# Transposing query weights straight from DRAM, modulation weights by columns, first key products in halves, and a new hand-written order

## The chip, the core and the metric

The kernel runs on one core of a Trainium2 chip. The core has TensorE (PE in the profile, its weight loads PEld), VectorE (DVE), ScalarE (ACT), GpSimd (POOL) and SyncE (SP), each working through its own queue of instructions in order, and 16 DMA engines that carry the transfers which SP (and at the very start ACT) issues. The metric is the device time of one execution in microseconds.

## What is computed

A transformer block with adaptive layer norm: linear attention with softmax features for 2,048 tokens of width 512 in 32 heads of 16, and a gated MLP of width 1,376. All inputs are bf16.

```python
mod = (_silu(c) @ w_mod).reshape(c.shape[0], 6, 1, -1)
sa, ca, ga, sb, cb, gb = ...
h = _layernorm(x) * (1 + ca) + sa
q, k, v = split(h @ wqkv)                          # 32 heads of 16
pq, pk = q @ w_phi, k @ w_phi                      # head by head
phi_q = concat(softmax(pq), softmax(-pq)); phi_k = concat(softmax(pk), softmax(-pk))
kv = einsum('bhsf,bhsd->bhfd', phi_k, v); z = phi_k summed over s
o = (phi_q @ kv) / (phi_q @ z + 1e-6)
x = x + ga * (o @ wo)
h = _layernorm(x) * (1 + cb) + sb
x = x + gb * ((sigmoid(h @ w_gate) * (h @ w_up)) @ w_down)
```

## The kernel before

Tokens are worked on in 16 tiles of 128. Nothing is scheduled at run time: every piece of work is a named task, and the text `ORDER` lists all tasks. The program is emitted in that order, so each engine's queue holds its own tasks in the order of the text. A suffix (`@A`, `@D`, `@P`) moves a task to ACT, DVE or POOL; without one it goes to the first engine that its `G.add` names. Buffers (eight PSUM banks, and slots for the larger SBUF tiles) are handed out in the order of the text too, so a task can wait for an earlier user of its bank.

The head of the kernel, with the names that the rest uses:

- **Loads** (`ld_...`, L664 to L687) stand in SP's queue. `ld_x0a` to `ld_x3a` bring the tokens, `ld_wk0/1`, `ld_wv0`, `ld_wq0` the three parts of `A_wqkv` into `wqk_sb` and `wv_sb`, `ld_wm00/01` the shift and scale columns (0 to 1,023) of `w_mod` for the first norm, each load with two of the four blocks of 128 rows; `ld_wmga` and `ld_wmm2` its other columns. In the built program a load is not issued before the eighth load ahead of it has landed. ACT issues two small loads, of `c` and `w_phi`.
- **Warm-up** (`warm0`, `warm1_0` to `warm1_15`, L720): matmuls on zeros that keep PE running while the loads come.
- **Norm of the tokens**: `st1_t` (statistics, DVE, L799), `rs1_g`, `nmr1_g`, `xn1_t` (normalized tile, L824 to L828). Tiles are grouped: group 0 is tile 0, group 1 tile 1, group 2 tiles 2 and 3, then two tiles to a group.
- **Transposes of the tokens**: `tphgj` (PE, L841) transposes column block j (of four) of group g, and `hm1_gj` (L848 on ACT, L850 on DVE or POOL) scales and shifts it into `h1T`. Groups 6 and 7 are transposed by DMA instead (`xT1_t`, L833). `hm1` needs the modulation column `modc`, which `modc1.0`, `modc1.1` (PE, 16 small matmuls each, L735) and `modc1c` (ACT, L741 and L742) make of the two loads.
- **Folded weights**: `w_phi` is multiplied into Wq and Wk once. For Wk, `tpw` (PE, L759) transposes, `wTc` (L763) copies into `wT_sb`, `fold1j` (L776) multiplies with the block-diagonal `bd`, `foldc1j` (L782, L784) copies to `wqk_f`. For Wq the transposes are DMAs (`wqT0` to `wqT3`, L769) from `wqk_sb`, then `fold0j`, `foldc0j`. In both, a fold waits for all four transposed blocks.
- **Keys and values**: `Kt` (four matmuls over the four blocks j, L867) and `Vt` (L871) of tile t; `et` (two exponentials, ACT, L883), `nt` (sums, DVE, L886), `rt` (reciprocal), `phit` (POOL or DVE, L889), `vat` (copy of the values, L907), `kvt` (eight matmuls that add tile t to `kvacc`, L280).
- **Queries**: `Qcb` (L945) and their exponentials `qecb` (L950), where the order finds room. `modca` (from `ld_wmga`, read back over DRAM as `gra`, and multiplied into `wo`) and `modc2` (from `ld_wmm2`) make the other modulation columns.

After the keys come `kvm`, `kvp`, `kvz`, `kvn`, the attention output per tile (`sm`, `num`, `u`, `o`, `oT`, `out`), the second norm, and the MLP in six chunks (`g`, `tg`, `u`, `hm`, L574 to L595; `y`, `fin`, `st`, L612 to L621).

In the order before, each engine's queue starts so (names as above; what is not needed is left out):

```
PE   warm0 c1 warm1_0..7 tpw1 tpw0 tpw3 warm1_8 tpw2 warm1_9..14 fold11 fold13 fold12 fold10 modc1.0 modc1.1 tph20 tph21 tph11
     tph22 warm1_15 tph03 tph23 tph10 tph01 tph00 K2 tph02 tph13 K3 tph12 tph33 tph30 K0 tph32 V2 K1 tph53 V3 tph52 tph31 modca.0 modca.1 V0 V4
SP   x0b x0a x1a wk0 wk1 x2a wm00 wm01 x2b wv0 x1b wq0 wd2 wmga x3a wqT2 wqT0 wqT3 wqT1 xT1_10 xT1_11 gwa wu1 wmm2 xT1_13 xT1_12 wg0 wo wu0 wd gra
```

Of the kernel before, what the change touches and what calls it, by code (L numbers as in the profile page):

```python
# [1133 lines left out]
```

## Time and profile before

| | us |
|---|---|
| median of 3 runs | 208.01 |
| lowest and highest | 207.98, 208.36 |
| the profiled execution | 208.63 |
| its span in the profile | 206.9 |

The profiled execution's own time is 1.7 us longer than the span from its first to its last instruction. The profile page gives the busy time of each engine, a strip of 40 slices, and the chain of waits: the work that ended last, followed back. The other views used are the busy time of each engine in chosen stages, what each engine waited for, the instructions in order of time (start, duration, engine, line, operation, output and inputs, count; in brackets the idle time before and what ended it), and the list of transfers (issuing queue, count, size, and the time from issue to landing).

### The profile page before, as it was taken

Reading aid. Unit: us, or ns where it says so; the run is one execution under the profiler, and the core shown is the slowest. Engines: PE = TensorE matmul, PEld = TensorE weight load, DVE = VectorE, ACT = ScalarE, POOL = GpSimd, SP = SyncE. Lnnn points to the kernel's source line nnn. Section 1 sums busy time; section 2 is a strip of 40 time slices with the busy share of each in tenths; the row PEclk is TensorE's granted clock in tenths of the full one; section 3 lists DMA queues with packets and bytes.
Section 4 is the critical chain, followed back from the end, with each engine's and each line's share of the span. In section 5 each row is a group of like instructions: output and inputs, shape, how many; then the busy total and the mean of one; then the engine's idle time right before and its main releaser. Section 6 shows DMA issues by size and latency. Waiting matters only on the chain.

```text
span 206.9 us, 4373 instructions
## 1 busy us (share of the span) xinstructions
PE 199.4 (96%) x1539; PEld 112.8 (54%) x1563; DVE 168.8 (82%) x462; ACT 110.1 (53%) x267; POOL 96.3 (47%) x128
## 2 busy tenths in 40 slices
PE   7889999999999999999999999999999999999993
PEld 2465554554676689768764544454444444444442
DVE  3999999998989998999999999898797865235632
ACT  2689999999979986433343543231523351144100
POOL 5787999999976987774256000014400220000000
PEclk9999999999999999999999999999999999999999
DMA  6999877697101211205321121141223022000111
...
DMA packets 32557, 19.27 MB, mean 93 GB/s; under 512 B 21169, under 2 KB 30738, under 8 KB 32530
## 3 DMA queue, kind: packets, MB, share of 16 engines
...
q8 instruction: 14, 0.23, 0.5%
q14 instruction: 13, 0.11, 0.2%
q10 hardware_dynamic: 530, 0.02, 0.1%
...
## 4 chain that ended last, share of the span: by engine, by line
PE 71%; ACT 18%; DMA 4%; DVE 3%; SPq 2%; issue 1%; DVEq 0%; ACTq 0%
PE y_ps L612 18%; PE u_ps L574 17%; PE g_ps L574 17%; ACT e L883 8%; PE a_ps L483 7%; PE q_ps L945 4%; ACT h1T L848 4%; DMA wmod_sb<-in_w_mod_dram 4%; ACT vaug L907 3%; PE num L366 2%; PE num L450 2%; DVE phi L889 1%; PE g_ps L576 1%; SPq L664 1%; DVE ks L886 1%
## 5 line engine op out<-in xcount | busy, mean ns | idle before, releaser
L584 ACT ACTIVATE tg<-g_ps 128x512 bf16<-128x512 f32 (+5 forms) x66 | 28.9, 454 | 58.0 <-PE g_ps L574 38.1
L612 PE MATMUL y_ps<-wd_sb,wmod_sb 128*128 128x512 bf16 (+4 forms) x184 | 43.8, 366 | 0.2
L595 DVE SCALAR_TENSOR_TENSOR wmod_sb<-tg,u_ps 128x512 bf16<-128x512 bf16 (+4 forms) x63 | 30.0, 494 | 15.0 <-ACT tg L584 7.3
L574 PEld LDWEIGHTS <-wu_sb 128*128 128x128 bf16 (+1 forms) x252 | 21.7, 99 | 15.7 <-issue 0.2
L574 PEld LDWEIGHTS <-wg_sb 128*128 128x128 bf16 (+1 forms) x252 | 21.5, 99 | 14.7 <-issue 0.2
L889 POOL TENSOR_TENSOR phi<-e,ks 128x1024 bf16<-128x1024 bf16 (+2 forms) x17 | 27.7, 1637 | 1.1 <-DVE ks L899 0.3
L612 PEld LDWEIGHTS <-wmod_sb 128*128 128x128 bf16 (+1 forms) x187 | 17.4, 98 | 16.9 <-issue 0.2
L574 PE MATMUL u_ps<-wT_sb,wu_sb 128*128 128x512 bf16 (+2 forms) x122 | 23.7, 321 | 0.1
L574 PE MATMUL g_ps<-wT_sb,wg_sb 128*128 128x512 bf16 (+2 forms) x122 | 23.7, 321 | 0.1
L503 POOL TENSOR_SCALAR ve<-mv 128x2 f32<-128x2 f32 (+1 forms) x8 | 1.8, 223 | 42.3 <-DVE mv L493 42.3
L574 PE MATMUL u_ps<-wqk_sb,wu_sb 128*128 128x128 bf16 (+4 forms) x127 | 19.9, 287 | 0.1
L886 DVE TENSOR_REDUCE ks<-e 128x64 f32<-128x1024 bf16 (+2 forms) x22 | 19.7, 903 | 0.3 <-ACT e L883 0.2
L574 PE MATMUL g_ps<-wqk_sb,wg_sb 128*128 128x128 bf16 (+4 forms) x127 | 19.6, 287 | 0.1
L883 ACT ACTIVATE e<-k_ps 128x512 bf16<-128x512 f32 (+2 forms) x44 | 18.4, 500 | 0.0
L950 ACT ACTIVATE eT<-q_ps 128x512 bf16<-128x512 f32 x32 | 16.8, 611 | 1.8 <-PE q_ps L945 1.7
L474 POOL TENSOR_TENSOR o<-u 128x512 bf16<-128x512 f32 x10 | 12.6, 1269 | 9.5 <-DVE u L456 4.2
L619 DVE TENSOR_TENSOR ot<-y_ps,x 128x512 bf16<-128x512 f32 (+2 forms) x17 | 11.2, 656 | 6.9 <-PE y_ps L612 6.6
L483 PE MATMUL a_ps<-wo_sb,oT 128*128 128x512 bf16 x57 | 15.7, 379 | 0.4
L945 PE MATMUL q_ps<-h1T,wqk_f 128*128 128x512 bf16 x62 | 15.7, 379 | 0.1
L867 PE MATMUL k_ps<-wqk_f,h1T 128*128 128x512 bf16 x63 | 15.5, 379 | 0.1
L871 PE MATMUL v_ps<-wv_sb,h1T 128*128 128x512 bf16 x59 | 15.2, 379 | 0.2
L799 DVE BATCH_NORM_STATS2 st<-x_sb 128x6 f32<-128x512 bf16 x16 | 10.8, 673 | 2.6 <-DMA x_sb<-in_A_x_dram 2.6
...
## 6 DMA issues: line engine op xcount, KB each, us to landing
...
wmod_sb<-in_w_mod_dram SPq DMA_DIRECT2D x3, 512.0 KB, 6.5
wmod_sb<-in_w_mod_dram SPq DMA_DIRECT2D x1, 1536.0 KB, 10.3
...
```

The costliest lines, as they stand in the source:

```text
L483: pe.matmul(ap_[:], lhsT=oT[:, j, :], rhs=wo_sb[:, j, :], start=(j == 0), stop=(j == KT - 1))
L574: pe.matmul(ps[:fsz, 0:n], lhsT=w[:, j, ft * P:ft * P + fsz], rhs=h[:, j, 0:n], start=(j == 0), stop=(j == KT - 1))
L584: G.add(f"tg{k}.{ft}", {"ACT": 0.13 + n * 0.00083}, lambda e, tg=tg, g_ps=g_ps, fsz=fsz, n=n: act.activation(tg[:fsz, 0:n], g_ps[:fsz, 0:n ...
L595: dve.scalar_tensor_tensor(hm_all[:fsz, hm[k].slot, ft, 0:n], tg[:fsz, 0:n], 1.0, u_ps[:fsz, 0:n], op0=ALU.add, op1=ALU.mult)
L612: mm = pe.matmul(y[:, 0:c1 - c0], lhsT=hm_all[:fsz, hm[k].slot, ft, tl * P:(tl + 1) * P], rhs=wd_sb[:fsz, ft, c0:c1], start=(ft == 0), sto ...
L867: pe.matmul(kp[:], lhsT=h1T[:, j, t * P:(t + 1) * P], rhs=wqk_f[:, j, D:2 * D], start=(j == 0), stop=(j == KT - 1))
L871: pe.matmul(vp[:], lhsT=h1T[:, j, t * P:(t + 1) * P], rhs=wv_sb[:, j, :], start=(j == 0), stop=(j == KT - 1))
L883: act.activation(ee[:, ha:hb, s, :], kp[:, ha * DH:hb * DH].rearrange("p (h j) -> p h j", j=DH), ACT.Exp, scale=1.0 - 2.0 * s)
L886: dve.tensor_reduce(ks[:, ha:hb].rearrange("p h s -> p (h s)"), ee[:, ha:hb].rearrange("p h s j -> p (h s) j"), axis=AX.X, op=ALU.add)
L889: engine(e).tensor_tensor(ph[:, ha * 32:hb * 32].rearrange("p (h j) -> p h j", j=DH), ee[:, ha:hb].rearrange("p h s j -> p (h s) j"), ks[: ...
L945: pe.matmul(qp[:], lhsT=wqk_f[:, j, blk * P:(blk + 1) * P], rhs=h1T[:, j, cq * 512:(cq + 1) * 512], start=(j == 0), stop=(j == KT - 1))
L950: act.activation(eT[cq][:, s * 4 + blk, :], qp[:], ACT.Exp, scale=1.0 - 2.0 * s)
```

## The change

- `DIRECT = [1, 0]`: the load of Wq into `wqk_sb` is gone. The four DMA transposes `wqT0` to `wqT3` read the rows of `A_wqkv` in DRAM. Wk is still loaded and transposed by PE.
- Wk is loaded in halves of rows, not of columns. `tpwk` transposes the four column blocks of row block k, and the copy `wTc` spreads them over `wT_sb`; a fold needs only the transposed block of its own number, for Wk and Wq.
- The modulation weights of the first norm come in four loads of 256 columns with all rows: `wm00a/b` (shift and scale columns of blocks 0 and 1), `wm01a/b` (blocks 2 and 3). `modc1.h` makes the columns of blocks 2h and 2h+1, `modc1c0` (on DVE in the order) and `modc1c1` (ACT) copy them, and `hm1_gj` needs only the half that has its j.
- `K0` to `K7` are tasks `a` (blocks 0 and 1) and `b` (blocks 2 and 3), `V0` to `V3` too. A half needs only its own `h1T` blocks.
- `wu` is loaded at once, and the whole `ORDER` is new: which engine takes a task as well. Of the tasks whose engine can be chosen, the main shifts are: ACT gets 2 more fold copies, 2 more reciprocals, 1 more value copy, 6 more z copies, and 2 fewer `xn1`, 2 fewer `xn2`, 1 fewer `wTc`; DVE gets 2 more `xn1` and 1 `wTc`, and 2 fewer fold copies, 2 fewer reciprocals, 1 fewer value copy, 6 fewer z, 3 fewer `o`; POOL gets 3 more `o` and 3 more `xn2`.

The queues start so after the change:

```
PE   warm0 c1 warm1_0..5 tpw0 warm1_6 tpw3 warm1_7 tpw1 warm1_8 fold10 tpw2 fold13 warm1_9 warm1_10 fold11 tph20 fold12 modc1.0 warm1_11 warm1_12
     tph23 tph00 warm1_13 warm1_14 tph13 tph01 tph12 tph21 warm1_15 tph11 tph10 modc1.1 tph22 K0a tph02 tph03 K3a K1a tph31 K1b tph32 tph30 K2a
     K0b K3b tph33 V2a V0a K2b tph50 tph52 V2b tph51 V0b K4a modca.0 V1a modca.1 V1b tph43 tph42 K4b
ACT  c2 rs1_2 rs1_1 wTc0 rs1_0 wTc1 wTc2 foldc10 foldc13 foldc12 foldc11 hm1_20 hm1_01 hm1_10 modc1c1 hm1_12 hm1_22 hm1_13 hm1_03 hm1_31 hm1_32 e1 e0 e3 va2 e2
SP   x0b x0a wk0 wk1 x1a wm00a wm00b x2a wm01a wm01b x1b x2b wv0 x3a wqT0 wd2 wmga wqT3 wqT2 wmm2 wqT1 gwa xT1_10 xT1_11 wg0 wd xT1_13 xT1_12 gwb grb wo gra wu0
```

The diff without the text of the order:

```diff
--- before.py
+++ after.py
@@ -32,55 +32,58 @@
-SPLIT = {"wk": 2, "wv": 1, "wq": 1, "wg": 1, "wu": 2, "x1": 2, "x2": 2, "x3": 1}
+KSP = 8
+DIRECT = [1, 0]
+VSP = 4
+SPLIT = {"wk": 2, "wv": 1, "wq": 2, "wg": 1, "wu": 1, "x1": 2, "x2": 2, "x3": 1}
 LETTER = {"A": "ACT", "D": "DVE", "P": "POOL"}
 ORDER = """
...
@@ -184,6 +187,7 @@
     mhalf = cst.tile([P, NT], FP32, name="mhalf")
+    mone = cst.tile([P, 2, 2], FP32, name="mone")
     st1 = cst.tile([P, NT, 6], FP32, name="st1")
@@ -241,6 +245,8 @@
     pool.memset(mhalf[:], -0.5)
+    pool.memset(mone[:, 0], 0.0)
+    pool.memset(mone[:, 1], 1.0)
     pool.memset(eps[:], 1e-5)
@@ -641,7 +647,7 @@
             dve.tensor_reduce(bst[:, 2:3], bsq[:, 4:8], axis=AX.X, op=ALU.add)
-        G.add("bndb", {"DVE": 1.2}, f_b, r=[("bnd", j) for j in range(KT)] + ["mod1"], w=["bst"])
+        G.add("bndb", {"DVE": 1.2}, f_b, r=[("bnd", j) for j in range(KT)] + [("mod1", 0), ("mod1", 1)], w=["bst"])
         ps = bank("bnd", [1, 3])
@@ -664,14 +670,16 @@
     def load_wm(i):
-        load(f"wm0{i}", [("wmod0", i)], lambda e: sp.dma_start(wmod_sb[:, 2 * i:2 * i + 2, 0:1024], wmod_v[:, 2 * i:2 * i + 2, 0:1024]), 512 * K1)
+        for s in range(2):
+            c = s * D + 256 * i
+            load(f"wm0{i}{'ab'[s]}", [("wmod0", i, s)], lambda e, c=c: sp.dma_start(wmod_sb[:, :, c:c + 256], wmod_v[:, :, c:c + 256]), 256 * K1)
     load_x("x0a", 0, 2)
-    for h in range(SPLIT["wk"]):
-        load(f"wk{h}", [("wk", h)], lambda e, a=D + D // SPLIT["wk"] * h, b=D + D // SPLIT["wk"] * (h + 1): sp.dma_start(wqk_sb[:, :, a:b], wqkv_v[:, :, a:b]), 512 * K1 / SPLIT["wk"])
+    for h in range(0 if DIRECT[1] else SPLIT["wk"]):
+        load(f"wk{h}", [("wk", h)], lambda e, a=KT // SPLIT["wk"] * h, b=KT // SPLIT["wk"] * (h + 1): sp.dma_start(wqk_sb[:, a:b, D:2 * D], wqkv_v[:, a:b, D:2 * D]), 512 * K1 / SPLIT["wk"])
     load_wm(0)
...
     load_x("x0b", 2, 4)
-    for w, dst, c0 in (("wv", wv_sb[:], 2 * D), ("wq", wqk_sb[:, :, 0:D], 0)):
+    for w, dst, c0 in (("wv", wv_sb[:], 2 * D), ("wq", wqk_sb[:, :, 0:D], 0))[:1 if DIRECT[0] else 2]:
         for h in range(SPLIT[w]):
@@ -737,37 +745,59 @@
 
-    def f_mc1(ps):
-        act.copy(modc[:, 0:4], ps[:, 0:4])
-        act.add(modc[:, 4:8], ps[:, 4:8], 1.0)
+    def modc1_task(h):
+        ps = bank("modc_ps", [P, 2, 2])
+        dst = modc[:, 0:8].rearrange("p (s j) -> p s j", s=2)[:, :, 2 * h:2 * h + 2]
+
+        def f(e):
+            for j in range(KT):
+                for s in range(2):
+                    for i in range(2):
+                        c = s * D + (2 * h + i) * P
+                        pe.matmul(ps[:, s, i:i + 1], lhsT=wmod_sb[:, j, c:c + P], rhs=sc_bf[:, j:j + 1],
+                                  start=(j == 0 and s == 0 and i == 0), stop=(j == KT - 1), skip_group_check=True)
+
+        def f2(e):
+            if e == "ACT":
+                act.copy(dst[:, 0], ps[:, 0])
+                act.add(dst[:, 1], ps[:, 1], 1.0)
+            else:
+                dve.tensor_tensor(dst, ps[:], mone[:], op=ALU.add)
+        G.add(f"modc1.{h}", {"PE": 0.4}, f, r=[("wmod0", h, 0), ("wmod0", h, 1), "scbf"], w=[("mc1ps", h)], bufs=[ps])
+        G.add(f"modc1c{h}", {"ACT": 0.35, "DVE": 0.15}, f2, r=[("mc1ps", h)], w=[("mod1", h)], bufs=[ps])
 
...
         act.add(modc[:, 12:16], ps[:, 4:8], 1.0)
-    modc_task("modc1", list(range(8)), [("wmod0", 0), ("wmod0", 1)], ["mod1"], f_mc1, 0.35)
+    for h in range(2):
+        modc1_task(h)
     modc_task("modca", list(range(8, 12)), ["wmod_ga", "wmod_ga"], ["gcola"], lambda ps: act.copy(gcol[:, 0:4], ps[:]), 0.2)
...
         for k in range(KT):
-            if side == 1:
+            if side == 1 and DIRECT[1]:
+                G.add(f"wkT{k}", {"SP": 1.2}, lambda e, k=k: sp.dma_start_transpose(wT_sb[:, 1, :, k * P:(k + 1) * P], A_wqkv[k * P:(k + 1) * P, D:2 * D]),
+                      w=[("wT", 1, k)], nbytes=-1)
+            elif side == 1:
                 tp = bank("tp_w", [P, 512], BF16)
...
                 def f(e, k=k, tp=tp):
-                    for kt_in in range(KT):
-                        pe.transpose(tp[:, kt_in * P:(kt_in + 1) * P], wqk_sb[:, kt_in, D + k * P:D + (k + 1) * P], ident[:])
+                    for h in range(KT):
+                        pe.transpose(tp[:, h * P:(h + 1) * P], wqk_sb[:, k, D + h * P:D + (h + 1) * P], ident[:])
 
                 def f2(e, k=k, tp=tp):
-                    if e == "ACT":
-                        act.copy(wT_sb[:, 1, k, :], tp[:])
-                    else:
-                        dve.tensor_copy(wT_sb[:, 1, k, :], tp[:])
+                    (act.copy if e == "ACT" else dve.tensor_copy)(wT_sb[:, 1, :, k * P:(k + 1) * P], tp[:].rearrange("p (h m) -> p h m", h=KT))
                 G.add(f"tpw{k}", {"PE": 0.24}, f, r=[("wk", k * SPLIT["wk"] // KT)], w=[("tpw", k)], bufs=[tp])
...
             else:
-                G.add(f"wqT{k}", {"SP": 1.2}, lambda e, k=k: sp.dma_start_transpose(wT_sb[:, 0, :, k * P:(k + 1) * P], wqk_sb[:, k, 0:D]),
-                      r=[("wq", k * SPLIT["wq"] // KT)], w=[("wT", 0, k)], nbytes=-1)
+                if DIRECT[0]:
+                    G.add(f"wqT{k}", {"SP": 1.2}, lambda e, k=k: sp.dma_start_transpose(wT_sb[:, 0, :, k * P:(k + 1) * P], A_wqkv[k * P:(k + 1) * P, 0:D]),
+                          w=[("wT", 0, k)], nbytes=-1)
+                else:
+                    G.add(f"wqT{k}", {"SP": 1.2}, lambda e, k=k: sp.dma_start_transpose(wT_sb[:, 0, :, k * P:(k + 1) * P], wqk_sb[:, k, 0:D]),
+                          r=[("wq", k * SPLIT["wq"] // KT)], w=[("wT", 0, k)], nbytes=-1)
         for kt_in in range(KT):
@@ -782,7 +812,7 @@
                     dve.tensor_copy(dst, ps[:])
-            G.add(f"fold{side}{kt_in}", {"PE": 0.24}, f3, r=[("wT", side, k) for k in range(KT)] + ["bd"], w=[("fold", side, kt_in)], bufs=[ps])
+            G.add(f"fold{side}{kt_in}", {"PE": 0.24}, f3, r=[("wT", side, kt_in), "bd"], w=[("fold", side, kt_in)], bufs=[ps])
             G.add(f"foldc{side}{kt_in}", {"ACT": 0.54, "DVE": 0.62}, f4, r=[("fold", side, kt_in)], w=[("wqk", kt_in, side)], bufs=[ps])
@@ -850,11 +880,11 @@
                 w = {"DVE": 0.171 + 0.035 * n, "ACT": 0.25 + 0.11 * n, "POOL": 0.12 + 0.165 * n}
-                G.add(f"hm1_{g}{j}", w, f_m, r=[("h1raw", t) for t in ts] + ["mod1"],
+                G.add(f"hm1_{g}{j}", w, f_m, r=[("h1raw", t) for t in ts] + [("mod1", j // 2)],
                       w=[("h1", g, j)], port=("POOL", "DVE"))
...
                 w = {"DVE": 0.08 + 0.115 * n, "ACT": 0.25 + 0.105 * n}
-                G.add(f"hm1_{g}{j}", w, f_m, r=[("tph", g, j), "mod1"], w=[("h1", g, j)], bufs=[tp])
+                G.add(f"hm1_{g}{j}", w, f_m, r=[("tph", g, j), ("mod1", j // 2)], w=[("h1", g, j)], bufs=[tp])
 
@@ -862,14 +892,19 @@
 
-        def f_k(e, t=t, kp=kp):
-            for j in range(KT):
+        def f_k(e, js=range(KT), t=t, kp=kp):
+            for j in js:
                 pe.matmul(kp[:], lhsT=h1T[:, j, t * P:(t + 1) * P], rhs=wqk_f[:, j, D:2 * D], start=(j == 0), stop=(j == KT - 1))
 
-        def f_v(e, t=t, vp=vp):
-            for j in range(KT):
+        def f_v(e, js=range(KT), t=t, vp=vp):
+            for j in js:
                 pe.matmul(vp[:], lhsT=h1T[:, j, t * P:(t + 1) * P], rhs=wv_sb[:, j, :], start=(j == 0), stop=(j == KT - 1))
-        G.add(f"K{t}", {"PE": 0.87}, f_k, r=h1k + [("wqk", j, 1) for j in range(KT)], w=[("k", t)], bufs=[kp])
+        if t < KSP:
+            for h in range(2):
+                js = (2 * h, 2 * h + 1)
+                G.add(f"K{t}{'ab'[h]}", {"PE": 0.435}, lambda e, js=js, f=f_k: f(e, js), r=[h1k[j] for j in js] + [("wqk", j, 1) for j in js], w=[("k", t)], bufs=[kp])
+        else:
+            G.add(f"K{t}", {"PE": 0.87}, lambda e, f=f_k: f(e), r=h1k + [("wqk", j, 1) for j in range(KT)], w=[("k", t)], bufs=[kp])
         ee = Buf("r2k", [P, H, 2, DH], BF16, "e")
@@ -902,7 +937,12 @@
             G.add(f"phi{t}.{a}", {"POOL": 0.08 + 1.77 * w, "DVE": 0.08 + 1.07 * w}, f_p, r=[("kr", t, a)], w=[("phi", t, a)], bufs=[ee, ks, ph], port=("POOL", "DVE"))
-        G.add(f"V{t}", {"PE": 0.87}, f_v, r=h1k + [("wv", h) for h in range(SPLIT["wv"])], w=[("v", t)], bufs=[vp])
+        if t < VSP:
+            for h in range(2):
+                js = (2 * h, 2 * h + 1)
+                G.add(f"V{t}{'ab'[h]}", {"PE": 0.435}, lambda e, js=js, f=f_v: f(e, js), r=[h1k[j] for j in js] + [("wv", h if SPLIT["wv"] == 2 else 0)], w=[("v", t)], bufs=[vp])
+        else:
+            G.add(f"V{t}", {"PE": 0.87}, lambda e, f=f_v: f(e), r=h1k + [("wv", h) for h in range(SPLIT["wv"])], w=[("v", t)], bufs=[vp])
         va = Buf("vaug", None, None, "va")
```

More of the change, by code (lines that the diff above doesn't have):

```diff
@@ new lines @@
+tph32 tph30 K2a K0b pmem xn1_9@P K3b hm1_32@A tph33 V2a V0a K2b e1.0 e0.0 ld_x3a wqT0 xn1_8@P tph50 hm1_30 hm1_33 rs1_4@P e3.0 tph52 nmr1_4 hm1_52 ld_wd2
+ld_wmga wqT3 V2b tph51 V0b rs1_6@P wqT2 K4a modca.0 V1a modca.1 xn1_6@P xn1_7@P ld_wmm2 wqT1 va2 e2.0 V1b tph43 tph42 K4b hm1_50 n0.0 nmr1_6 xn1_10@P hm1_51@A
+tph41 modcac r0.0@A va1 hm1_43@A st1_13 n1.0 tph53 V5 va0 K5a xn1_11@P phi0.0 tph40 hm1_42 hm1_53 st1_12 r1.0@A hm1_41@A e4.0 hm1_40 gwa n2.0 xT1_10 xT1_11
+va5 V4 r2.0 V3a V3b kv0.0 fold03 K5b va4 foldc03 rs1_7 fold02 K7a phi1.0 n3.0 kv1.0 foldc02 e5.0 r3.0@A ld_wg0 phi2.0 nmr1_7 n4.0 va3@D K6a K6b fold00 K9
```

88 lines of the change are left out of this document (42 added, 46 removed).

## The prediction, before the result was known

> **What bounds the kernel now.** I read the page first, then the busy time of each engine by stage, then what PE waited for, then the chain of waits.
>
> ```profile
> span 206.9 us, 4373 instructions
> PE 199.4 (96%) x1539; PEld 112.8 (54%) x1563; DVE 168.8 (82%) x462; ACT 110.1 (53%) x267; POOL 96.3 (47%) x128
> ```
>
> ```profile
> 0.00:12.20 12.20, 9.69 (x90) 5.10 (x90) 8.31 (x27) 6.54 (x15) 7.82 (x29) 1.00 0.85 270
> 12.20:20.00 7.80, 7.69 (x75) 4.62 (x73) 7.33 (x25) 7.59 (x20) 6.52 (x11) 1.00 1.22 284
> 20.00:30.00 10.00, 9.89 (x89) 5.83 (x90) 9.86 (x18) 9.94 (x25) 9.77 (x8) 1.00 0.75 123
> 30.00:40.00 10.00, 9.68 (x77) 5.09 (x78) 9.69 (x21) 9.94 (x24) 9.52 (x10) 1.00 0.71 221
> 40.00:50.00 10.00, 9.95 (x76) 5.08 (x76) 9.23 (x20) 9.86 (x33) 9.69 (x8) 1.00 1.04 368
> 50.00:56.00 6.00, 5.67 (x78) 3.49 (x77) 5.61 (x10) 5.71 (x15) 5.78 (x8) 1.00 0.16 57
> 56.00:203.80 147.80, 146.80 (x1072) 83.53 (x1089) 118.57 (x348) 60.50 (x141) 47.22 (x60) 1.00 0.18 42
> 203.80:206.90 3.10, 0.00 (x0) 0.00 (x0) 0.23 (x1) 0.00 (x0) 0.00 (x0) 0.94 0.16 45
> ```
>
> The columns are stage, length, busy PE, PEld, DVE, ACT, POOL, granted clock, DMA share, GB/s. From 12.2 us to 203.8 us PE idles 0.11 + 0.11 + 0.32 + 0.05 + 0.33 = 0.92 us up to 56 and 1.00 us after it. The closing 3.10 us (last addition, last store) are untouched. The clock is full. So the end is the time at which PE becomes dense, plus its work, plus 1.9 us. The order can win only in the head and in that 1.9. ACT is as full as PE from 20 to 50 us; relieving ACT pays only as far as PE idles.
>
> ```profile
> PE modc_ps L735 <- DMA wmod_sb<-in_w_mod_dram: 0.5, 1, 0.5
> PE kvacc L280 <- POOL phi L889: 0.3, 1, 0.3
> ```
>
> ```profile
> 4.45 7.29 DMA wmod_sb<-in_w_mod_dram
> 11.79 0.57 PE modc_ps L735 x16
> 12.65 3.19 ACT h1T L848 x8
> 15.83 2.92 ACT e L883 x6
> ```
>
> The chain says what sets the dense start: the second half of the modulation weights lands at 4.45 + 7.29 = 11.74, modc1.1 runs at 11.79, and only then can any h1T be scaled.
>
> **The head: loads.** In both orders modc1.1 needs ten units of 256 KB from SP's queue (four x, two of Wk, four of the modulation weights); only order and run length differ.
>
> ```profile
> 7.06 0.62 PE L759 MATMUL tp_w<-ident,wqk_sb 128*128 128x128 bf16 x8 [0.57 <-DMA wqk_sb<-in_A_wqkv_dram]
> 7.89 0.40 PE L759 MATMUL tp_w<-ident,wqk_sb 128*128 128x128 bf16 x4 [0.21 <-DMA wqk_sb<-in_A_wqkv_dram]
> 9.05 0.69 DVE L799 BATCH_NORM_STATS2 st<-x_sb 128x6 f32<-128x512 bf16 x1 [0.19 <-DMA x_sb<-in_A_x_dram]
> 7.74 0.55 SPq L676 DMA_DIRECT2D wqk_sb<-in_A_wqkv_dram  x1
> wqk_sb<-in_A_wqkv_dram SPq DMA_DIRECT2D x1, 512.0 KB, 8.6
> ```
>
> A Wk half (runs of 256 columns, 512 B) lands 7.89 - 7.06 = 0.83 us after the other. The four modulation units, in runs of 2 KB, follow x at 9.05 and end at 11.74: 0.67 each. Between 11.74 and the landing of Wq at 7.74 + 8.6 = 16.34 come 1,536 KB in runs of 1 KB: 0.77 per unit. After the change the modulation units have 512 B runs, 4 x (0.83 - 0.67) = +0.64, and Wk 1 KB runs, 2 x (0.77 - 0.83) = -0.12. So modc1.1 starts 0.52 later, at 12.31. Bounds: 0 (if the runs were not the cause) and 1.04 (twice it); I take 0.52, the price of the same shape.
>
> The Trainium skill, DMA: Bandwidth & Descriptors, section "Why small descriptors are slow (HBM only)", speaks against the column split: about three cycles are lost per packet, so by an estimate from it 512 B (16 beats and 3) costs 1.13 times 2 KB. The trace's 0.83 against 0.67 is 1.24 times, dearer than the rule; by the rule the four units would add 0.36 and the sum below would be 0.28 lower.
>
> **The head: what PE has done by then.** Behind modc1.1 stood 13 transposes and a warm-up matmul; now 12 transposes of groups 0 to 2 and that matmul (warm1_15) stand ahead of it.
>
> ```profile
> 12.20 0.55 PE L841 MATMUL tp_h<-ident,xn 128*128 128x128 bf16 x7
> L841 PE MATMUL tp_h<-ident,xn x28: 216/219/219, 12.2 to 19.2; 128*128 128x128 bf16 x28
> 13.49 0.81 PE L867 MATMUL k_ps<-wqk_f,h1T 128*128 128x512 bf16 x3
> 21.88 1.89 PE L867 MATMUL k_ps<-wqk_f,h1T 128*128 128x512 bf16 x8
> L867 PE MATMUL k_ps<-wqk_f,h1T 128*128 128x512 bf16 x63 | 15.5, 379 | 0.1
> ```
>
> A transpose takes (0.55 - 0.219) / 6 = 0.055, a 512-column matmul (1.89 - 0.379) / 7 = 0.216, half a key tile 0.43. Moved ahead: 12 x 0.055 + 0.216 = 0.88. Also, from 11.79 + 0.55 to the first key matmul at 13.49 lie 1.15 us, for work of 13 x 0.055 + 0.216 = 0.93: PE lost 0.22 waiting for the first h1T. In the new order modc1.0 needs seven of the ten units: the same five that were in at 7.89, and two at 0.83, so 9.55; h1T 0 and 1 of groups 0 to 2 are scaled before modc1.1 ends, and K0a, K3a, K1a are ready. The head is worth 0.52 - 0.88 - 0.22 = **-0.58**.
>
> The halves by themselves buy less than their name: K0a stands behind modc1.1 on PE, so no key product starts before the second half of the weights is there. They add no matmul and save only that 0.22. ACT must be through by then: three copies of transposed Wk, four of the fold, three h1T:
>
> ```profile
> 7.50 1.07 ACT L763 COPY wT_sb<-tp_w 128x512 bf16<-128x512 bf16 x2 [0.81 <-PE tp_w L759]
> 10.28 1.56 ACT L782 CAST wqk_f<-fold_ps 128x512 bf16<-128x512 f32 x3
> ```
>
> 3 x 0.54 + 4 x 0.52 + 3 x 0.40 = 4.9, with one rs1 about 5.4, from about 7: ends at 12.4, before modc1.1 does (12.86). Cost nothing; there is 0.4 of cover. The fourth copy and the first modc column go to DVE, the two memsets for it to POOL ahead of bd: covered by the same wait for loads.
>
> **After the head: the wait that may come.** Wq's load goes; its four transposes read DRAM. wqT0 now stands in SP's queue ahead of the load for modca (wmga), and x3a too.
>
> ```profile
> 19.30 0.66 PE L735 MATMUL modc_ps<-sc_bf,wmod_sb 128*128 128x1 bf16 x16
> 13.00 0.35 SPq L789 DMA_DIRECT2D wd_sb<-in_B_w_down_dram  x1
> 13.39 0.42 SPq L681 DMA_DIRECT2D wmod_sb<-in_w_mod_dram  x1
> wmod_sb<-in_w_mod_dram SPq DMA_DIRECT2D x1, 512.0 KB, 5.6
> 16.38 5.29 SPq L769 DMA_TRANSPOSE wT_sb<-wqk_sb  x4
> wT_sb<-wqk_sb SPq DMA_TRANSPOSE x1, 5.3
> 23.60 1.06 PE L776 MATMUL fold_ps<-bd,wT_sb 128*128 128x128 bf16 x16
> ```
>
> wmga landed at 13.39 + 5.6 = 18.99. The first transpose landed at 16.38 + 5.3 = 21.68 and all four were there for the fold at 23.60: at most 1.9 / 3 = 0.64 each. New: modulation in at 12.26, then x1b, x2b, wv, x3a (6 units, 4.6), wqT0 (0.6), then wd2 and wmga, 608 KB: 1.8 at 0.77 a unit, 2.65 as they took before (16.34 to 18.99). So wmga lands between 19.3 and 20.1. PE reaches modca.0 at 12.31 + 0.55 + 18 transposes (1.0) + 13 half tiles (5.6) = 19.5. The wait, none at 19.30 before, is 0 to 0.6; V1a, V1b, K4b stand behind it. I take **+0.3**. A read from DRAM is not in the trace; below 0.64 it cannot help here, the upper end is in the rivals.
>
> wmm2 (1,536 KB) is issued only after modca.1, and wqT1, gwa, xT1_10, xT1_11, wg stand behind it on SP.
>
> ```profile
> 24.96 0.43 SPq L686 DMA_DIRECT2D wu_sb<-in_B_w_up_dram  x1
> wmod_sb<-in_w_mod_dram SPq DMA_DIRECT2D x1, 1536.0 KB, 10.3
> 29.48 0.55 POOL L850 TENSOR_SCALAR h1T<-h1T,modc 128x256 bf16<-128x256 bf16 x1
> ```
>
> Before, 2,144 KB took from 24.96 to 35.8 (issued 25.5), 1.3 a unit. From 20.8 wmm2 ends at 25.4 (0.77) to 28.6 (1.3); three transposes at 0.6 bring xT1_11 in between 27.2 and 30.4. Group 6 is first scaled at about the old time, 29.5. I take 0.
>
> **Engine shares in the key stage.** ACT loses two xn, one qe and three h1T before the last e, gains one fold copy, one modc2 copy and a reciprocal; DVE loses two fold copies and a va, POOL a phi (phi5 goes to DVE). Each is relieved; PE can gain at most its idle 0.92. I take a third, **-0.3**, between 0 and -0.92. After 56 us DVE hands three o additions to POOL and six z copies to ACT; the 1.00 us of PE idle there is 0.07 in ten us, with no wait named but small ones: 0. wu as one load behind ga's has 21 us of cover:
>
> ```profile
> 52.79 0.34 SPq L920 DMA_DIRECT2D ga_sb<-gdr  x1
> 74.32 0.89 PE g_ps L574 x16
> ```
>
>
> **Sum.** -0.58 + 0.3 - 0.3 = -0.58 on the profiled run's own 208.63 us gives 208.05; the median of the runs is 0.62 below that run, so **207.4 us**.
>
> **The rivals.**
> - Given back (0.20): wmga waits the full 0.6 and the relief is nothing: +0.02, 208.0. For it: wmga's 18.99 left only 0.3 before. Against it: wd2 need not be slow again.
> - Slower through SP's queue (0.20): wmm2 at 1.3 a unit and 0.6 late with modca puts xT1_11 at 31.0; ACT stands 1.5 at hm1_60, with foldc01, e7 and qe00 behind it, and PE behind the banks and Q00 that these hold: -0.58 + 0.6 + 1.5 = +1.5, 209.5; it decides from a landing after 29.5 on. For it: that pace was measured. Against it: transposes and wu1 shared the rings then.
> - Transposes from DRAM slow (0.10): at three times 0.64 each, wmga comes 1.3 later still: -0.58 + 0.6 + 1.3 = +1.3, 209.3. No row of before speaks on it.
> - More (0.10): no wait at modca, all 0.92 and half of the 1.00 regained: -0.58 - 0.92 - 0.5 = -2.0, 206.0.
>
> **How the numbers follow.** My forecast has 0.40; its own range is 206.8 to 207.6. Two runs differ by about 0.2%, 0.4 us. Faster: 0.40 + 0.10 = 0.50; same 0.20; slower 0.20 + 0.10 = 0.30. The range 206.3 to 209.2 leaves out the lowest half of "more" and the upper parts of the two slow cases.
>
> **What would show it.** Right: modc1.1 near 12.3 with 12 transposes ahead of it; K0a at once behind it; PE at modca waiting under 0.6; PE idle from there to 56 us below 0.9. Wrong: modc1.1 before 11.8 or after 12.8; a PE wait on DMA over 0.6 at modca or at fold0; ACT waiting for xT1; or a stage after 56 us whose PE idle differs from 1.0 by more than 0.4.

## The result

| | before | after |
|---|---|---|
| median, us | 208.1 (207.98 to 208.36) | 214.7 (213.45 to 215.98) |
| ratio to before, 95% interval | | 1.0314, 1.0255 to 1.0373 |
| the profiled execution | 208.63 | 213.45 |
| its span | 206.9 | 211.7 |

The change costs 6.6 us, where the prediction had -0.6 with a range up to 209.2. The profiled execution of after is the shortest of its four, so the two profiles show 4.8 us of the 6.6.

The first lines of the page, after:

```profile
span 211.7 us, 4368 instructions
PE 201.1 (95%) x1538; PEld 113.4 (54%) x1563; DVE 169.9 (80%) x452; ACT 110.2 (52%) x276; POOL 100.9 (48%) x134
```

The shares hardly moved; where the time went is seen by stages (the columns are stage, length, busy PE, PEld, DVE, ACT, POOL, granted clock, DMA share, GB/s):

```profile
12.20:20.00 7.80, 7.05 (x57) 3.82 (x58) 7.62 (x25) 7.59 (x19) 7.53 (x18) 1.00 1.23 263
20.00:30.00 10.00, 9.85 (x88) 5.82 (x91) 9.16 (x17) 8.59 (x24) 8.66 (x7) 1.00 0.90 251
30.00:40.00 10.00, 8.55 (x111) 5.03 (x109) 9.93 (x15) 9.22 (x25) 7.68 (x6) 1.00 0.98 259
40.00:50.00 10.00, 8.01 (x55) 4.22 (x57) 8.65 (x13) 5.78 (x19) 6.98 (x6) 0.83 0.27 79
...
60.00:208.00 148.00, 146.84 (x1060) 83.37 (x1074) 115.70 (x338) 61.62 (x147) 54.47 (x68) 1.00 0.20 50
...
42.30:45.60 3.30, 3.08 (x11) 1.32 (x13) 3.23 (x5) 0.59 (x1) 1.55 (x1) 0.56 0.57 178
45.60:48.00 2.40, 2.40 (x22) 1.46 (x21) 1.33 (x2) 1.05 (x2) 2.40 (x3) 0.90 0.00 0
```

Three stages lost: from 12.2 to 20 us PE idles 0.75 (0.11 before), from 30 to 40 it idles 1.45 (0.32 before), and from 40 to 50 it idles 1.99 (0.05 before) and its clock is granted at 0.83, down to 0.56 between 42.3 and 45.6. From 60 us on nothing is lost. PE's longest waits between 12 and 62 us:

```profile
PE tp_h L871 <- DVE xn L856: 1.7, 1, 1.7
PE kvacc L286 <- POOL phi L924: 1.4, 1, 1.4
PE modc_ps L743 <- DMA wmod_sb<-in_w_mod_dram: 0.7, 1, 0.7
```

The chain of waits, from 4 to 46 us, runs through VectorE in just that stretch:

```profile
5.64 6.47 DMA wmod_sb<-in_w_mod_dram
...
12.74 7.26 DMA wmod_sb<-in_w_mod_dram
...
31.33 2.09 DVE h1T L880
...
39.11 3.10 DVE xn L856 x2
```

These are xn1_14 and xn1_15, and hm1_62 and hm1_61 before them. In the order of time, with GpSimd beside them:

```profile
29.40 3.93 POOL L924 TENSOR_TENSOR phi<-e,ks 128x1024 bf16<-128x1024 bf16 x2 [0.51 <-ACT ks L932]
29.44 1.21 DVE L921 TENSOR_REDUCE ks<-e 128x64 f32<-128x1024 bf16 x1
31.06 2.36 DVE L880 TENSOR_SCALAR h1T<-h1T,modc 128x256 bf16<-128x256 bf16 x2
33.34 1.20 DVE L921 TENSOR_REDUCE ks<-e 128x64 f32<-128x1024 bf16 x1
...
38.12 3.93 POOL L924 TENSOR_TENSOR phi<-e,ks 128x1024 bf16<-128x1024 bf16 x2
39.03 3.17 DVE L856 TENSOR_SCALAR xn<-x_sb,mv,rs 128x512 bf16<-128x512 bf16 x2
40.10 0.43 PE L286 MATMUL kvacc<-vaug,phi 128*128 128x68 bf16 x8 [1.40 <-POOL phi L924]
42.25 0.23 PE L871 MATMUL tp_h<-ident,xn 128*128 128x128 bf16 x1 [1.67 <-DVE xn L856]
```

And the same line of instructions by itself, with the like in the kernel before:

```profile
L856 DVE TENSOR_SCALAR xn<-x_sb,mv,rs x3: 381/1162/2081, 9.9 to 40.1; 128x512 bf16<-128x512 bf16 x3
```

```profile
29.63 0.99 DVE L850 TENSOR_SCALAR h1T<-h1T,modc 128x256 bf16<-128x256 bf16 x3
```

An xn on VectorE took 0.381 us in the head, 1.16 and 2.08 here; two hm1 from SBUF to SBUF took 2.36, where three took 0.99 before, while no phi ran on GpSimd. Three of the slow ones end 0.09 to 0.15 us after a phi of GpSimd does: of the two phi from 38.12 the first ends near 40.05 and the second at 42.05, xn1_14 ends at 39.03 + 1.16 = 40.19 and xn1_15 at 42.20; the second phi from 29.40 ends at 33.33 and hm1_61 at 33.42. The phi keep their 1.93, and a reduction beside a phi (29.44) takes what it takes with none (33.34). Not everything on VectorE is slow there: an hm1 that reads PSUM took 0.40 beside a phi in the kernel before (at 40.91). So it looks as if an operation from SBUF to SBUF on bf16 is held until GpSimd's ends; e10 below tests it. The Trainium skill, SBUF — State Buffer, section "Who interferes with whom", states this: VectorE and GpSimd share one pair of SBUF ports, a scalar operation in a two-port mode needs it, and whoever has it keeps it for the whole instruction, while reductions never need it. The rows agree.

PE's other wait of that stretch, 1.40 us at kvacc, is for phi6, which stands behind rs1_8 on GpSimd. The first instruction of rs1_8 waits 2.16 us for statistics that VectorE makes behind the two slow hm1, and then it is slow itself:

```profile
36.24 1.11 POOL L839 TENSOR_SCALAR ve<-mv 128x2 f32<-128x2 f32 x1 [2.16 <-DVE mv L830]
36.07 1.21 DVE L924 TENSOR_TENSOR phi<-e,ks 128x1024 bf16<-128x1024 bf16 x1
```

It takes 1.11 and ends at 37.35, 0.07 after phi5, which the new order gives to VectorE; with no phi on VectorE beside it the same instruction takes 0.22, in the kernel before and in e9. In e1, e6 and e10, beside the same phi5, it takes 1.11 again. So it looks as if GpSimd is held by a phi of VectorE as well; no run was made for this alone.

The start of the dense stretch, PE's and ScalarE's in the order of time, and kvm, which ends the key stage:

```profile
11.87 0.80 PE L757 MATMUL modc_ps<-sc_bf,wmod_sb 128*128 128x1 bf16 x16
12.64 0.59 PE L897 MATMUL k_ps<-wqk_f,h1T 128*128 128x512 bf16 x2
15.37 2.08 ACT L918 ACTIVATE e<-k_ps 128x512 bf16<-128x512 f32 x4
...
18.71 0.59 PE L897 MATMUL k_ps<-wqk_f,h1T 128*128 128x512 bf16 x2
20.05 0.43 PE L743 MATMUL modc_ps<-sc_bf,wmod_sb 128*128 128x1 bf16 x8 [0.74 <-DMA wmod_sb<-in_w_mod_dram]
21.20 0.37 SPq L689 DMA_DIRECT2D wmod_sb<-in_w_mod_dram  x1
...
L307 DVE TENSOR_TENSOR kvm<-kvacc,mask x2: 430/436/442, 60.8 to 61.1; 128x272 bf16<-128x272 f32 x2
```

```profile
L301 DVE TENSOR_TENSOR kvm<-kvacc,mask x2: 429/435/441, 55.8 to 56.3; 128x272 bf16<-128x272 f32 x2
```

The last is the kernel before. kvm starts at 60.8 us, at 55.8 before: +5.0. The terms in these profiles: head -0.33 (the first exponential starts at 15.37; in the same view of the kernel before, at 15.70), modca +0.74, phi 1.40 - 0.3 = +1.1, xn1_15 +1.67, clock 10 x (1 - 0.83) = +1.7. Sum +4.88. The two longest executions of after lost more to the clock: over the span it was granted at a mean of 0.981 and 0.980 there and of 0.992 in the other two, which by (1 - clock) x span is 4.1 to 4.3 us and 1.7 us, an estimate.

### The profile page after: what moved, and what is told of

Read it like the earlier page. It is cut to its first block, busy times and chain, and to the rows that moved or that the text cites. A ratio compares the mean times of both kernels' runs of the same rounds, so it can differ in the third digit from the quotient of the medians.

```text
span 211.7 us, 4368 instructions
## 1 busy us (share of the span) xinstructions
PE 201.1 (95%) x1538; PEld 113.4 (54%) x1563; DVE 169.9 (80%) x452; ACT 110.2 (52%) x276; POOL 100.9 (48%) x134
## 4 chain that ended last, share of the span: by engine, by line
PE 66%; DVE 18%; DMA 6%; ACT 3%; issue 2%; SPq 2%; DVEq 0%; ACTq 0%
PE y_ps L618 15%; PE g_ps L580 14%; PE u_ps L580 14%; DMA wmod_sb<-in_w_mod_dram 6%; PE a_ps L489 5%; PE q_ps L985 5%; DVE ks L921 3%; PE v_ps L901 3%; ACT e L918 2%; DVE wmod_sb L601 2%; PE k_ps L897 2%; PE num L372 2%; DVE xn L856 1%; PE num L456 1%; PE g_ps L582 1%
## 5 line engine op out<-in xcount | busy, mean ns | idle before, releaser
L590 ACT ACTIVATE tg<-g_ps 128x512 bf16<-128x512 f32 (+5 forms) x66 | 28.6, 454 | 52.0 <-PE g_ps L580 28.6
L618 PE MATMUL y_ps<-wd_sb,wmod_sb 128*128 128x512 bf16 (+3 forms) x182 | 42.6, 366 | 0.1
L924 POOL TENSOR_TENSOR phi<-e,ks 128x1024 bf16<-128x1024 bf16 (+2 forms) x17 | 26.3, 1554 | 5.6 <-DVE ks L934 2.4
L480 POOL TENSOR_TENSOR o<-u 128x512 bf16<-128x512 f32 x13 | 16.5, 1274 | 17.3 <-DVE u L447 10.1
L580 PE MATMUL g_ps<-wT_sb,wg_sb 128*128 128x512 bf16 (+2 forms) x122 | 23.2, 321 | 0.1
L580 PE MATMUL u_ps<-wT_sb,wu_sb 128*128 128x512 bf16 (+2 forms) x122 | 22.9, 321 | 0.1
L580 PE MATMUL g_ps<-wqk_sb,wg_sb 128*128 128x256 bf16 (+4 forms) x128 | 19.2, 287 | 0.0
L918 ACT ACTIVATE e<-k_ps 128x512 bf16<-128x512 f32 (+2 forms) x44 | 17.9, 507 | 1.3 <-PE k_ps L897 1.2
L901 PE MATMUL v_ps<-wv_sb,h1T 128*128 128x512 bf16 x61 | 17.1, 401 | 0.3 <-issue 0.2
L897 PE MATMUL k_ps<-wqk_f,h1T 128*128 128x512 bf16 x61 | 16.3, 379 | 0.2
```

Of the source, the lines that this page charges most:

```text
L580: pe.matmul(ps[:fsz, 0:n], lhsT=w[:, j, ft * P:ft * P + fsz], rhs=h[:, j, 0:n], start=(j == 0), stop=(j == KT - 1))
L590: G.add(f"tg{k}.{ft}", {"ACT": 0.13 + n * 0.00083}, lambda e, tg=tg, g_ps=g_ps, fsz=fsz, n=n: act.activation(tg[:fsz, 0:n], g_ps[:fsz, 0:n ...
L618: mm = pe.matmul(y[:, 0:c1 - c0], lhsT=hm_all[:fsz, hm[k].slot, ft, tl * P:(tl + 1) * P], rhs=wd_sb[:fsz, ft, c0:c1], start=(ft == 0), sto ...
L897: pe.matmul(kp[:], lhsT=h1T[:, j, t * P:(t + 1) * P], rhs=wqk_f[:, j, D:2 * D], start=(j == 0), stop=(j == KT - 1))
L901: pe.matmul(vp[:], lhsT=h1T[:, j, t * P:(t + 1) * P], rhs=wv_sb[:, j, :], start=(j == 0), stop=(j == KT - 1))
L918: act.activation(ee[:, ha:hb, s, :], kp[:, ha * DH:hb * DH].rearrange("p (h j) -> p h j", j=DH), ACT.Exp, scale=1.0 - 2.0 * s)
```

## The experiments

**The two xn1 off VectorE (e1), and the hm1 too (e2).** In the order of after (of the order only the stretch that changes is shown, here and below):

```diff
-K10 xn1_14@D xT1_12 xn1_15@D kv6.0
+K10 xn1_14@A xT1_12 xn1_15@A kv6.0
```

> The changed kernel with xn1_14 and xn1_15 on ACT instead of DVE. Port theory: these two DVE operations took 1.16 and 2.08 us beside phi on POOL, against 0.38 alone, PE then idled near 40 to 46 us and its granted clock was 0.56 there; off DVE, the two cost ACT 0.81 each where it idles, PE idle of 40 to 50 us (1.99) falls below 0.8, the clock stays at 1.0, and the time falls by 2.5 to 4 us from 214.7 to 210.7 to 212.2. Queue theory (the late load for modc2 and what stands behind it on SP is the cause): the time stays within 1 us of 214.7, and PE idles elsewhere instead.

Measured: 210.43 us, ratio to before 1.0103 (1.0074 to 1.0131): 4.3 us less than after. The granted clock is full again, in all four executions:

```profile
40.00:50.00 10.00, 9.43 (x83) 5.14 (x84) 8.73 (x18) 9.60 (x31) 9.92 (x9) 1.00 0.27 79
```

> As the run before, and hm1_62 and hm1_61 on ACT too (on DVE the second took 2.09 us beside phi3 and phi4 on POOL, against 0.33 in the kernel before). Port theory: a further 0.5 to 1.5 us, 209.5 to 211. If only DVE's time near 40 us decides: the same as the run before, within 0.4, since ACT pays 0.55 for each. Queue theory: within 1 us of 214.7.

e2 moves hm1_62 and hm1_61 to ScalarE as well: 211.13 us, 1.0134 (1.0097 to 1.017). No further gain, where the port theory had 0.5 to 1.5 us: ScalarE is busy 9.82 of the 10 us from 30 to 40, and PE now waits 1.1 us for the two xn1 there and 1.0 for a copy of ScalarE.

**The same edit made to the kernel before (e4).** xn1_14 (ScalarE) and xn1_15 (GpSimd) go to VectorE, nothing else:

```diff
-xn1_14
+xn1_14@D
...
-xn1_15@P
+xn1_15@D
```

> The kernel before with xn1_14 (ACT) and xn1_15 (POOL) on DVE, nothing else. Port theory: beside phi on POOL each takes 1 to 2 us instead of 0.38, DVE falls behind by 1.5 to 3 us and PE idles: 209.5 to 211.5. If the operations are slow only in the changed kernel's order: DVE pays 0.8, ACT and POOL win as much, 207.7 to 208.5.

Measured: 210.79 us, 1.0132 (1.0091 to 1.0172), 2.6 more than the kernel before beside it (208.21). The line of xn and PE's wait:

```profile
L826 DVE TENSOR_SCALAR xn<-x_sb,mv,rs x3: 310/382/1398, 10.9 to 39.7; 128x512 bf16<-128x512 bf16 x3
...
PE tp_h L841 <- DVE xn L826: 2.0, 1, 2.0
```

Two words of the order cost the old kernel 2.6 us. The time is the expected one, the account only half: xn1_14 took 1.40 and ended at 37.23, 0.15 after the phi beside it, but xn1_15 ran with GpSimd idle and took 0.31. It starts only at 39.73, since it stands behind four other operations in VectorE's queue, which the slow xn1_14 had already made late, and PE waits 2.0 us for it. So the loss here is one held operation and the queue behind it. The clock was full in the profiled execution (210.37) and at a mean of 0.992 in two of the other three; in after, all four have lost clock on top.

**No phi beside xn1_15 (e10).** VectorE's r7.0, which lets GpSimd start phi7, goes behind xn1_15; everything else is after, xn1 on VectorE included:

```diff
-nmr1_8 r7.0 va7 V10 kv5.0 K10 xn1_14@D xT1_12 xn1_15@D kv6.0
+nmr1_8 va7 V10 kv5.0 K10 xn1_14@D xT1_12 xn1_15@D r7.0 kv6.0
```

> This is the changed kernel with one move: VectorE's reading of K7 (r7.0), which frees GpSimd to start phi7, stands behind xn1_15 on VectorE instead of ahead of it, so that no phi runs on GpSimd while xn1_15 runs. Theory A (a VectorE operation from SBUF to SBUF is held while GpSimd runs a phi): xn1_14 still ends with phi6, but xn1_15 then takes about 0.38 us instead of 2.08, and TensorE's wait for it falls from 1.7 to under 0.6; phi7 starts about 0.5 us later. The time falls by about 1 us or more, to 212.5 or below, if the wait that goes is not given back at phi7. Theory B (the operation is slow for another reason, its operands or its place in the queue): xn1_15 stays above 1 us with GpSimd idle, and the time stays at 214 or above.

Measured: 211.16 us, 1.0136 (1.0119 to 1.0153), 3.5 us less than after. VectorE and GpSimd in the order of time, and the line of xn:

```profile
38.33 1.95 DVE L856 TENSOR_SCALAR xn<-x_sb,mv,rs 128x512 bf16<-128x512 bf16 x2
...
37.88 1.93 POOL L924 TENSOR_TENSOR phi<-e,ks 128x1024 bf16<-128x1024 bf16 x1
40.88 3.81 POOL L924 TENSOR_TENSOR phi<-e,ks 128x1024 bf16<-128x1024 bf16 x2 [1.08 <-DVE ks L934]
...
L856 DVE TENSOR_SCALAR xn<-x_sb,mv,rs x3: 381/404/1626, 10.0 to 39.9; 128x512 bf16<-128x512 bf16 x3
```

xn1_14 still takes 1.63 and ends 0.15 us after phi6, which ends at 37.88 + 1.93 = 39.81; xn1_15, with GpSimd idle, takes 0.40 in place of 2.08. It is the same operation, still directly behind xn1_14, and what runs beside it differs: theory A, as expected. PE's wait at xn is gone altogether; its waits for a phi of GpSimd rise from 1.4 to 2.1. The granted clock stays full from 40 to 50 us, so the 3.5 us hold both the wait and the clock that was lost behind it.

**Loads.** e3 takes ld_wmm2 behind xT1_11 in SP's queue; e6 is e1 with ld_wmga ahead of ld_x3a.

```diff
-ld_x3a wqT0 ... ld_wd2 ld_wmga wqT3
+ld_wmga ld_x3a wqT0 ... ld_wd2 wqT3
```

> The changed kernel with the load for modc2 (1,536 KB) moved behind xT1_11 on SP, as the kernel before had it, so that wqT1, xT1_10 and xT1_11 do not stand behind it. Queue theory: group 6 is scaled earlier and the time falls by 1.5 us or more, to 213 or less. Port theory: the two slow DVE operations stay; the time moves by under 1 us, or rises where modc2.0 on PE (32.1 us) now waits for the load (about 32.3).

> The first run's kernel (xn1_14 and xn1_15 on ACT, 210.4) with the load for modca moved ahead of x3a on SP. Wait theory: PE no longer waits at modca (1.1 us in that run) and the time falls by 0.6 to 1.1, to 209.3 to 209.8. If the key stage is bound by POOL's phi and not by that wait: under 0.3 us, and the wait turns up at kvacc.

e3: 213.06 us, 1.0211 (1.017 to 1.0253); the wait at xn stays 1.7 and the span is 212.1. The order of the big load is not what holds VectorE. What its place costs by itself is undecided: the median is 1.6 us below after's, about what the queue theory had, while the profiled span is 0.4 longer and e3's executions lost less clock (means of 0.992 to 1.000). e6: 209.61 us, 1.0056 (1.0032 to 1.008), 0.8 less than e1, though the intervals touch: the wait at modca (1.1 in e1) is gone and PE is busy all of 12.2 to 20 us. What is left there is 1.4 for a phi of GpSimd.

**Query weights straight from DRAM, by itself (e5).** The kernel before without ld_wq0, its four DMA transposes reading DRAM, its order otherwise kept.

> The kernel before with one part of the change alone: no load of Wq, its four transposes read DRAM, order otherwise as it was. If transposes from DRAM are as cheap as from SBUF: 207.6 to 208.6 (208.1 before), with 512 KB less in the rings near 16 us. If they are slow and block the rings (my rival): the load for modca or the folds come late and the time rises by 0.8 us or more.

Measured: 208.47 us against 208.36, ratio 1.000 (0.998 to 1.0019). The list of transfers:

```profile
wT_sb<-in_A_wqkv_dram SPq DMA_TRANSPOSE x4, 4.5
...
wT_sb<-wqk_sb SPq DMA_TRANSPOSE x4, 4.2
```

The second line is the kernel before. The median from issue to landing is 4.5 us from DRAM and 4.2 from SBUF. In the old kernel the part that gives the change its name neither costs nor brings anything. In after, where other loads run beside them, the same four took 6.8.

**What holds the phi of GpSimd (e7, e9).** In e6 GpSimd waits 2.2 us at rs1_8 for the statistics st1_14 and st1_15, which stand behind hm1_61 on VectorE. e7 is e6 with rs1_8 on ScalarE; e9 is e6 with the two statistics ahead of hm1_62.

> As the run before, and rs1_8 on ACT instead of POOL, where it waits 2.2 us for DVE's last statistics with phi6 behind it (PE waits 1.5 us at kvacc for phi6). If that queueing is the rest of the loss: a further 0.8 to 1.5 us, 208.0 to 208.8. If phi6 waits for DVE's reciprocal anyway: under 0.3.

> This is e6_wmga_early with the two statistics st1_14 and st1_15 moved on VectorE from behind hm1_61 to ahead of hm1_62. In e6 rs1_8 on GpSimd still waited 2 us for these statistics, with phi6 queued behind it, and TensorE waited 1.4 us for phi6. Theory A (the rest of the loss is VectorE work held beside a GpSimd phi: hm1_62 and hm1_61 take 2 us, the statistics come that much late, and so rs1_8 and phi6): GpSimd's wait at rs1_8 falls under 0.5 us, TensorE's at phi6 under 0.5 us, and the time falls by about 1 us from e6's 209.6 to 208.0 to 208.6. Theory B (GpSimd itself has too much to do in 28 to 42 us, the wait for statistics only fills time that it would stand anyway): TensorE's wait at phi6 stays above 1 us and the time stays at 209.4 or more. If hm1_62 and hm1_61 are late now instead, TensorE waits at the first product of hidden tiles 61 and 62, and the time stays at 209.4 or more as well.

e7: 211.1 us, 1.0124 (1.0074 to 1.0173), not the gain that was expected but 1.5 more than e6: phi6 now waits for VectorE's phi5 instead, and rs1_8 holds ScalarE's queue, so that the two xn1 come late. e9: 209.38 us, 1.0053 (1.0036 to 1.007). Its PE waits:

```profile
PE tp_h L871 <- ACT xn L854: 1.3, 2, 0.8
```

The wait for the phi went as theory A said, yet the time fell by 0.2, which is within the intervals, and not by 1: 1.3 us came back at the next place, the two xn1 in ScalarE's queue.

**Following that wait (e11, e15).** e11 is e9 with nmr1_8 earlier and the two xn1 on ScalarE directly behind e8.0 and behind the va6 that follows it; e15 is e9 with nmr1_8 earlier, xn1_14 one place ahead of qe00 on ScalarE, and xn1_15 left to GpSimd between phi6 and phi7. The edit of e11:

```diff
-n7.0 rs1_8@P kv4.0 Q00 V7 phi6.0 va11 e8.0 va6 qe00 nmr1_8
+rs1_8@P nmr1_8 n7.0 kv4.0 Q00 V7 phi6.0 va11 e8.0 xn1_14@A va6 xn1_15@A qe00
...
-K10 xn1_14@A xT1_12 xn1_15@A kv6.0
+K10 xT1_12 kv6.0
```

> This is e9_st_early with nmr1_8 on VectorE ahead of n7.0, and with xn1_14 and xn1_15 on ScalarE four and three places ahead (behind e8.0). In e9 TensorE's only waits over 0.3 us between 12 and 60 us were 1.3 us for these two, which stood in ScalarE's queue behind four other steps. Theory A (what is left of the loss is that lateness alone, and with it gone the changed order keeps what it gains in the head, about 0.6 us): TensorE waits under 0.4 us in all at 38 to 42 us, and the time falls by about 1.2 us to 207.9 to 208.5, level with the kernel before or a little under it. Theory B (ScalarE is full there, 9.8 of 10 us busy, and the steps that are now behind hold TensorE in their place): the time stays at 209.0 or more, with TensorE waiting for Vaug or eT or the next e.

> This is e9_st_early with nmr1_8 ahead of n7.0 on VectorE, xn1_14 on ScalarE one place ahead of qe00, and xn1_15 on GpSimd between phi6 and phi7, as the kernel before has it. Theory A (the 1.3 us that TensorE waits at these two in e9 is what is left of the loss): TensorE's wait there falls under 0.4 us and the time to 208.0 to 208.7. Theory B (the stage's three other engines have no room, so a wait removed here comes back at the next exponential, as in e11): 209.0 or more, with a wait of 1 us or more for an e, a phi or a copy between 40 and 46 us.

e11: 210.25 us, 1.0094 (1.0061 to 1.0126); e15: 210.33 us, 1.0116 (1.0079 to 1.0153). Theory B both times, though part of e15's time is the clock: its three executions at a mean of 0.992 took 210.73 to 211.40, the three at 1.000 took 208.79 to 209.92. PE's longest wait in e11 and what ScalarE waited for:

```profile
PE q_ps L985 <- ACT e L918: 1.8, 1, 1.8
...
ACT h1T L878 <- DMA h1T<-xn: 0.7, 1, 0.7
```

With the xn1 early, ScalarE stands at hm1_72 for a DMA transpose, with e10.0 behind it and PE behind that. Three edits, and the wait went from GpSimd's phi to ScalarE's xn to ScalarE's e.

**The halves (e8, e12), and the new head before the old order (e13, e14).** e8 is e7 with K0 to K7 and V0 to V3 whole, e12 the same of e11. e13 has the order of after up to K2b, e1.0 and e0.0, and behind it all other tasks in the order and on the engines of before; e14 is e13 with whole products.

> As the run before, with K0 to K7 and V0 to V3 whole again, each at the place of its second half. By the prediction's sum the halves save the 0.22 us of PE waiting for the first h1T, and K0a, K3a, K1a fill PE from 12.6 to 13.9: without them PE waits there, 0.3 to 1.3 us slower than the run before. If the halves are worth nothing: within 0.3 of it.

> This is e11_xn_ahead with the first eight key products and the first four value products whole again (K0 to K7 and V0 to V3, each at the place of its second half). Theory A (the halves let TensorE begin 0.5 us or more earlier, as the prediction had it): 0.4 to 1.0 us above e11, with TensorE's busy time in 12.2 to 20 us lower by about that. Theory B (what the halves bring at the head is given back later, since another engine ends the stage): within 0.3 us of e11.

> This has the head of the changed kernel (all tasks up to K2b, e1 and e0: loads by columns, Wk by rows, first products in halves, new order of the transposes, query weights transposed from DRAM) and behind it all other tasks in the order and on the engines of the kernel before (K0 to K3 and V0 to V3 in halves, two loads of the up weights). Theory A (the prediction's first term is real: PE begins its dense stretch 0.5 us earlier, and with the old order behind it nothing takes that back): 207.5 to 208.0, 0.4 to 0.8 under the kernel before. Theory B (the stage from 20 to 45 us is set by ScalarE, VectorE and GpSimd together, which the head brings nothing): within 0.3 us of the kernel before, with TensorE waiting about 0.5 us more between 20 and 56 us. It may also be slower, by 0.5 us or more, if the seam itself makes a wait, which would show as one wait of TensorE right behind K2b, before 24 us.

> This is e13_new_head with K0 to K3 and V0 to V3 whole. Theory A (the halves themselves start TensorE's products earlier): 0.3 to 0.7 us above e13, with TensorE's busy time from 12.2 to 20 us lower by that. Theory B (the halves bring nothing that lasts, as e12 against e11 had it): within 0.2 us of e13.

e8: 211.98 us, 1.0161 (1.0097 to 1.0224), which overlaps e7's interval: undecided. e12: 210.12 us, 1.0084 (1.0058 to 1.011), level with e11. The stages of e11, then of e12:

```profile
12.20:20.00 7.80, 7.60 (x70) 4.52 (x71) 7.63 (x24) 7.44 (x19) 7.38 (x18) 1.00 1.18 276
...
40.00:50.00 10.00, 8.11 (x69) 4.41 (x70) 7.20 (x17) 9.20 (x31) 7.53 (x7) 1.00 0.26 79
```

```profile
12.20:20.00 7.80, 6.94 (x68) 4.00 (x68) 7.63 (x23) 7.24 (x19) 7.55 (x18) 1.00 1.19 262
...
40.00:50.00 10.00, 8.80 (x71) 4.75 (x72) 7.74 (x18) 9.82 (x33) 7.73 (x8) 1.00 0.28 79
```

Whole products idle PE by 7.60 - 6.94 = 0.66 more in the head, and by 8.80 - 8.11 = 0.69 less later. e13: 209.87 us, 1.0113 (1.009 to 1.0135); e14: 209.69 us, 1.0099 (1.0078 to 1.012). The halves are worth nothing there either, and the new head in front of the old order makes it slower by 2.4, which neither theory had. PE in e13, in the order of time, and then in the kernel before:

```profile
18.45 0.67 PE L699 MATMUL modc_ps<-sc_bf,wmod_sb 128*128 128x1 bf16 x16
...
21.38 0.34 PE L827 MATMUL tp_h<-ident,xn 128*128 128x128 bf16 x3 [0.52 <-POOL xn L814]
...
28.04 0.68 PE L242 MATMUL kvacc<-vaug,phi 128*128 128x68 bf16 x16 [0.49 <-POOL phi L880]
28.56 1.02 PE L857 MATMUL v_ps<-wv_sb,h1T 128*128 128x512 bf16 x4
```

```profile
28.19 1.02 PE L871 MATMUL v_ps<-wv_sb,h1T 128*128 128x512 bf16 x4
```

At modca e13 is ahead by 19.30 - 18.45 = 0.85 us, so the new head brings PE there earlier. Then PE waits 0.52 for an xn and 0.49 for a phi, both of GpSimd, and at 28.56 it is 0.37 behind; the first is the wait before 24 us that the expectation allowed for where the two orders meet. At kvm it is 0.5 behind (56.3 for 55.8), at the end of the span 0.8 (207.7). That is less than the 2.4 of the medians: the kernel before measured 207.49 beside e13, and its profile is of an execution of 208.63.

No version of the new order beats the kernel before; the nearest is e9, 1.1 us above it.

## Why the prediction was wrong

- **The head, -0.58: a gain, as forecast, but a smaller one and not the end's.** modc1.1 started at 11.87, waited inside for the weights until 12.11 (forecast: landing at 12.26) and K0a followed at 12.64. Its end moved by 12.67 - 12.34 = +0.33, where +0.52 was taken. The first exponential came 0.33 earlier. But e13 shows that even 0.85 is gone by 28 us.
- **modca, +0.3:** +0.74, above the bound of 0.6 and a sign of being wrong by the prediction's own list; wmga landed at 20.0, inside 19.3 to 20.1, and PE was there at about 19.3 (18.71 + 0.59), 0.2 earlier than worked out.
- **ld_wmm2, 0:** the load itself was as worked out: 6.7 us by the list of transfers, from 21.20 to 27.9, inside 25.4 to 28.6. Whether its place costs anything is undecided (e3).
- **Engine shares in the key stage, -0.3 "between 0 and -0.92": the step that failed.** It counted instructions moved between engines and concluded that each is relieved and PE can only gain. It took two xn off ScalarE and a phi off GpSimd, and named for VectorE only what it loses: the two xn1 and the phi5 that VectorE takes over had no price. The order puts the two xn1 beside phi6 and phi7 on GpSimd, and there they took 1.16 and 2.08 us, where one takes 0.381 in the head. With both off VectorE 4.3 of the 6.6 us are gone (e1), with phi7 kept away from xn1_15 alone 3.5 (e10). Lost clock is part of both, 1.7 to 4.3 us an execution in after by the estimate above and none in e1; it had no term in the sum either. A gain was its bound on one side and zero on the other; a loss had no bound, and none was excluded by a row.
- **After 56 us, 0:** right: from kvm to the end of the span 211.7 - 60.8 = 150.9 us, 206.9 - 55.8 = 151.1 before.
- **The reading of what bounds the kernel** fell with it. PE idles 0.92 us up to 56, so the end was taken as the dense start plus PE's work. The rows quoted with it show DVE, ACT and POOL at 9.2 to 9.9 of 10 from 20 to 50 us too. Four engines in step have no slack; whichever comes late makes PE wait, as e2, e7, e9, e11 and e15 each show at another place.
- **The rivals:** the one on SP's queue named the right side by another mechanism, which did not come (ACT did not stand at hm1_60). Slow transposes from DRAM cost nothing in e5, and in after wmga landed inside its range all the same. "Given back" was right for modca, and for the head in e12 and e13, and too mild.

Still open: the 1.1 us between e9 and the kernel before belong to no single edit that was tried, and what phi5 on VectorE costs by itself was not run.
